# Summing the last output in four column tiles of one bank, with a single output transfer

## The chip, the cores and the metric

One core of one Trainium2 chip. The metric is device time in microseconds (us) of one execution, median over runs. The profile's span, from the first instruction to the last, is about 1.2 us shorter than the device time.

Some words: PE multiplies matrices and sums in PSUM; DVE, ACT and POOL compute on tiles; SP and ACT each have a queue on which they start transfers. The issue is the instruction that starts a transfer, a packet is one piece of it (one row, in the output transfers), the receipt is the increment of a semaphore that says that data has landed. An eviction copies a sum out of PSUM. The tail is the time from the landing of the last weights to the last receipt.

## The reference, cut to what matters

A decode step with a batch of four. An attention over a key and value cache and a small MLP both feed one output of 4 x 576; the MLP ends in a product with w4 (4608 x 576).

```python
xn = _layernorm(x)
# A: q from xn, softmax over the last 2048 keys of the cache, then @ wo
# B: x1 = xn + gather(gelu(_layernorm(xn) @ w1)) @ w2
#    h2 = _gelu(_layernorm(x1) @ w3) @ w4
return x + A(xn, ...) + (x1 + h2)          # [4, 1, 576], bf16
```

What the kernel loads is 88.5 MB, and the last 2048 keys and values of the two caches are 67 MB of it.

## The kernel before

Everything but the small x, which ACT loads, is loaded once, in one long series of transfers on the queue of SP. w4 comes last, in five pieces of 18, 9, 6, 2 and 1 rows per partition, so that the work after the last byte is small. All that goes into the output is summed in two PSUM accumulators of 4 x 288, in column tiles 0 and 32 of the PE array and in two banks; two engines evict them and two queues send them.

```python
W4_ROWS = (18, 9, 6, 2, 1)
out_sb = sb("out_sb", [36, D], BF16)
ACC = [ps[32 * k:32 * k + B, k, 0:HALF] for k in range(2)]      # HALF = 288
...
# output: two transfers of four rows of 576 B, one on either queue
for h, eng in ((0, "sp"), (1, "act")):
    ev_o[h] = add_dma([(o2[:, HALF*h:HALF*(h+1)], out_sb[32*h:32*h+B, HALF*h:HALF*(h+1)])], ("out", h),
                      [f"fin{h}"], 10000, engine=eng)
...
def acc_mm(e, h, lhsT, rhs, start=False, stop=False):
    return e.matmul(ACC[h], lhsT=lhsT, rhs=rhs, start=start, stop=stop, tile_position=(0, 32*h), skip_group_check=True)
...
# one piece of w4: for every row two matmuls of 4 x 288, after its landing
for t in range(t0, t1_):
    for h in hs:
        ins = acc_mm(e, h, h2T_sb[:, t, :], w4tile[t][:, HALF*h:HALF*(h+1)], stop=(t == 35))
...
add("dve", ... tensor_copy(out=out_sb[0:B, 0:HALF], in_=ACC[0]), waits=["MOl0"], sig="fin0")
add("act", ... activation(out=out_sb[32:32+B, HALF:D], in_=ACC[1], func=Copy), waits=["MOl1"], sig="fin1")
```

Of the kernel before, what the change touches and what calls it, by code (L numbers as in the profile page):

```python
# [6 lines left out]
FP32 = mybir.dt.float32  # L7
BF16 = mybir.dt.bfloat16
ACTF = mybir.ActivationFunctionType
# [26 lines left out]
def bass_parallel_sum__sliding_block_cached__mixer_s_mlp__decode_kernel(  # L36
    nc, A_x, A_k_cache, A_v_cache, A_wq, A_wo, B_x, B_w1, B_w2, B_w3, B_w4, out
):
    B, Sq, D = A_x.shape
# [14 lines left out]
    HALF = D // 2  # L54
# [3 lines left out]
    o2 = out.rearrange("b s d -> (b s) d")  # L58

    with ExitStack() as ctx:  # L60
        def sb(name, shape, dt):
            return ctx.enter_context(nc.sbuf_tensor(name, shape, dt))
# [44 lines left out]
        h2T_sb = sb("h2T_sb", [128, 36, B], BF16)  # L107
# [7 lines left out]
        ident_f = sb("ident_f", [128, 128], FP32)  # L115
# [12 lines left out]
        OTy = sb("OTy", [128, B, 32], BF16)  # L128
        ORT = sb("ORT", [128, B, 32], BF16)
        t1 = sb("t1", [B, D], FP32)  # L130
        out_sb = sb("out_sb", [36, D], BF16)

        ps = ctx.enter_context(nc.psum_tensor("ps", [128, 8, 512], FP32))[:]
        Sps = ps[:, 0:4, :]
        tb = [ps[:, 4 + k, :].bitcast(BF16).rearrange("p (t d) -> p t d", t=8) for k in range(4)]
        ACC = [ps[32 * k:32 * k + B, k, 0:HALF] for k in range(2)]
        ORps = ps[:, 2, 0:128]
        rinvps = ps[:, 3, 0:128]
        OTps = ps[:, 6, 0:32]
# [4 lines left out]
        H2Ta = ps[:, 7, :].bitcast(BF16)  # L144
        H2Tb = ps[:, 6, :].bitcast(BF16)[:, 0:128]
# [11 lines left out]
        def add(engine, emit, waits=(), sig=None, key=0.0, inc=(), loop=None, cond=None):  # L157
            seqc[0] += 1
            prog[engine].append(Op(emit, waits, sig, key, seqc[0], inc, loop, cond))

        def tok(nm):
            if nm not in S:
                S[nm] = sem("t_" + "_".join(str(k) for k in (nm if isinstance(nm, tuple) else (nm,))))
            return nm
# [6 lines left out]
        def add_dma(pairs, skey, waits=(), key=0.0, engine="sp"):  # L171
            tok(skey)
            dma_count[skey] = dma_count.get(skey, 0) + 16 * len(pairs)

            def emit(e):
                for o_, i_ in pairs:
                    e.dma_start(o_, i_).then_inc(S[skey], 16)  # L177
            add(engine, emit, waits, None, key)
            return ("dma", skey, dma_count[skey])
# [6 lines left out]
        KT = KV + 40.0  # L186


        P = lambda *a, **k: add("pool", *a, **k)

        def pool_ident(t, tag, pattern, view, key):
            P(lambda e: e.memset(t[:], 1.0), sig=tag + "1", key=key)
            P(lambda e: e.affine_select(out=view, in_=view, compare_op=ALU.is_equal, fill=0.0, base=0,
                                        pattern=pattern, channel_multiplier=1), waits=[tag + "1"], sig=tag, key=key + 0.5)
# [8 lines left out]
        pool_ident(perm_bf, "perm_bf", [[-1, NU], [-NU, NI]], perm_bf[:].rearrange("p (u i) -> p u i", u=NU), -95)  # L203
        pool_ident(permT_bf, "permT_bf", [[-1, NI], [-NI, NU]], permT_bf[:].rearrange("p (i u) -> p i u", u=NU), -95)
        pool_ident(ident_f, "ident_f", [[-1, 128]], ident_f[:], -94)
        P(lambda e: e.memset(hs_inT[:], 0.0), sig="hs_inT", key=-90)
        P(lambda e: e.memset(qs_dummy[:], 0.0), waits=["qs_zero"], inc=[(tok("qs"), 1)], key=-88)
        P(lambda e: e.memset(ones_f[:], 1.0), sig="ones_f", key=-89)
# [3 lines left out]
            waits=["ident_f"], sig="mU", key=-8)  # L212
# [25 lines left out]
        w4tile, w4cols, ev_w4, W4N = [], [], [], []  # L238
# [8 lines left out]
                w4cols.append((base + r, base + 128 * rc, rc))  # L247
            base += 128 * rc
        assert len(w4tile) == 36 and base == F
        ev_o = [None, None]  # L250
        for h, eng in ((0, "sp"), (1, "act")):
            ev_o[h] = add_dma([(o2[:, HALF * h:HALF * (h + 1)], out_sb[32 * h:32 * h + B, HALF * h:HALF * (h + 1)])], ("out", h),
                              [f"fin{h}"], 10000, engine=eng)
            add(eng, lambda e: None, [ev_o[h]], None, 10001)


        def ln_ops(idx, src, dst, first_waits, tag, k0):
# [61 lines left out]
        for b in range(B):  # L319
            add("dve", lambda e, b=b: e.tensor_copy(out=qp_out[:, b], in_=qp_in[:, b]), waits=["qTp", "qpad_zero"],  # L320
                sig="qT" if b == B - 1 else None, key=-29.4)
# [25 lines left out]
        def evac(n):  # L347
            if n % 8 in ACT_EVAC:
                return "act", lambda e: e.activation(out=ktbuf[:, n % 16], in_=tb[n % 4], func=ACTF.Copy)  # L349
            return "dve", lambda e: e.tensor_copy(out=ktbuf[:, n % 16], in_=tb[n % 4])  # L350
# [14 lines left out]
        for c in range(NC):  # L365
            lp = ("K", c // NPOS)
            for k in range(NBLK):
                w = [take(("k", c % NPOS), 16)] if k == 0 else []
                prev = (k + 4) % 8
                w.append(evtok(prev))  # L370
                add("pe", pe_T(NBLK * c + k), waits=w, sig=f"T{NBLK * c + k}", key=NBLK * c + k, loop=lp)
                eng, f = evac(NBLK * c + k)
                add(eng, f, waits=[f"T{NBLK * c + k}"] + ([f"SC{c - 2}"] if c >= 2 else []), inc=[("evA" if eng == "act" else "evD", 1)],
                    key=NBLK * c + k + 0.2)
            add("pe", pe_SC(c - 1), waits=[take("qs")], sig=f"SC{c - 1}", key=NBLK * c + SC_AFTER + 0.5, loop=lp)
            b, gq = CH[c]
            cc = 4 * b + gq
            P(lambda e, c=c, cc=cc: e.tensor_copy(out=Qs[:, c % NPOS, :], in_=Qpad_t[:, 128 * cc:128 * cc + 128]),  # L378
              waits=["qT", "qs_zero"] + ([f"SC{c - NPOS}"] if c >= NPOS - 1 else []), inc=[("qs", 1)], key=c)
# [6 lines left out]
            waits=["rmax"], sig="negb", key=KS + 0.05)  # L386
        for q in range(4):
            add("act", lambda e, q=q: e.activation(out=P_sb[:, q, :], in_=Sps[:, q, :], func=ACTF.Exp,
                                                   bias=negb[:, 0:1], scale=scale, accum_out=rs4[:, q:q + 1]),
                waits=["negb"], sig=f"exp{q}", key=KS + 0.1 + 0.01 * q)  # L390

        for q in range(4):
# [3 lines left out]
                waits=[f"PTx{q}", "permT_bf"] + (["PT0"] if q == 3 else []), sig=f"PTy{q}", key=k0)  # L396
            add("act", lambda e, q=q: e.activation(out=PT_t[:, 512 * q:512 * (q + 1)], in_=ps[:, 4 + q % 3, :], func=ACTF.Copy),
                waits=[f"PTy{q}"], sig=f"PT{q}", key=k0 + 0.16)
# [3 lines left out]
            waits=["rinv", "ident_f"], sig="diag", key=KS + 0.82)  # L402
        add("pe", lambda e: e.matmul(rinvps, lhsT=ones_f[:], rhs=diag[:], start=True, stop=True), waits=["diag", "ones_f", "exp3"],
            sig="rinvp", key=KS + 0.9)
        add("dve", lambda e: e.tensor_copy(out=rinvB[:].rearrange("p (c u e) -> p c u e", u=NU, e=2),
                                           in_=rinvps.rearrange("p (u c e) -> p c u e", u=NU, e=2)),
            waits=["rinvp"], sig="rinvB", key=KS + 1.5)
# [20 lines left out]
        for c in range(NC):  # L428
            w = [f"PV{c - 2}"] if c >= 2 else [f"PT{q}" for q in range(4)] + ["mU_bf1"]
            b, gq = CH[c]  # L430
            add("dve", dve_pad(c), waits=w, inc=[(tok("pad"), 1)], key=KV + 2 * max(c - 1, 0) + 0.2)
            add("pe", pe_PV(c), waits=[take("pad"), take(("v", c % NPOS), 16)] + ([take("otn")] if b == 0 else []), sig=f"PV{c}",
                key=KV + 2 * c, loop=("V", gq))
            if b == B - 1:
                hv = lambda t, gq=gq: t[:, 0:128].rearrange("p (b h) -> p b h", b=B)[:, :, 8 * gq:8 * gq + 8]
                add("dve", lambda e, hv=hv: e.tensor_tensor(out=hv(OTn), in0=OTps.rearrange("p (b h) -> p b h", b=B), in1=hv(rinvB), op=ALU.mult),  # L436
                    waits=["rinvB", f"PV{c}"], sig=f"OTn{gq}" if gq == 3 else None, inc=[(tok("otn"), 1)] if gq < 3 else [], key=KV + 2 * c + 0.1)


        def acc_mm(e, h, lhsT, rhs, start=False, stop=False):  # L440
            return e.matmul(ACC[h], lhsT=lhsT, rhs=rhs, start=start, stop=stop, tile_position=(0, 32 * h), skip_group_check=True)  # L441

# [8 lines left out]
        def pe_AO(half):  # L451
# [10 lines left out]
            waits=["OTy"], sig="ORp", key=KT - 2.5)  # L462
# [34 lines left out]
        for h in range(2):  # L497
# [3 lines left out]
                waits=[f"hs{h}", "ln1"], sig="x1" if h else "x1a", key=-29 + 0.6 * h)  # L501
# [4 lines left out]
        for h in range(2):  # L506
            add("act", lambda e, h=h: e.activation(out=h_sb[:, HALF * h:HALF * (h + 1)], in_=HTps[h], func=ACTF.Gelu_apprx_tanh),
                waits=[f"hT{h}", "x1nT"], sig="gelu_h" if h else None, key=-0.69 + 0.01 * h)

        segs = []  # L510
        for g in range(4):
            t = 9 * g
            while t < 9 * g + 9:
                n = next(m for m, (a, z) in enumerate(W4N) if a <= t < z)
# [18 lines left out]
        for k in range(3):  # L533
            add("act", lambda e, k=k: e.activation(out=h2g[:, 9 * XS[k]:9 * XS[k + 1]], in_=H2ps[k], func=ACTF.Gelu_apprx_tanh), waits=["h2_3"],
                sig="gelu2" if k == 2 else None, key=-0.9 + 0.1 * k)

        def pe_h2T(e):
# [3 lines left out]
            return ins  # L541
        add("pe", pe_h2T, waits=["gelu2"], sig="h2T", key=-0.6)
        h2o = h2T_sb[:].rearrange("p (g j) b -> p g j b", g=4)
        add("act", lambda e: e.activation(out=h2o[:, :, 0:8, :], in_=H2Ta.rearrange("p (j g y) -> p g j y", j=8, g=4)[..., 0:B], func=ACTF.Copy),
            waits=["h2T"], inc=[("evA", 1)], key=-0.3)
        add("dve", lambda e: e.tensor_copy(out=h2o[:, :, 8, :], in_=H2Tb.rearrange("p (g y) -> p g y", g=4)[..., 0:B]),
            waits=["h2T"], inc=[("evD", 1)], key=-0.3)

        last_p = len(W4N) - 1
        for n, (t0, t1_) in enumerate(W4N):  # L550
            def f(e, t0=t0, t1_=t1_, hs=(0, 1), n=n):
                ins = None
                for t in range(t0, t1_):
                    for h in hs:
                        ins = acc_mm(e, h, h2T_sb[:, t, :], w4tile[t][:, HALF * h:HALF * (h + 1)], stop=(t == 35))
                return ins
            if n < last_p:
                add("pe", f, waits=[ev_w4[n]], sig=f"MO{n}", key=KT + 20 + n)
            else:
                for h in range(2):  # L560
                    add("pe", lambda e, f=f, h=h: f(e, hs=(h,)), waits=[ev_w4[n]], sig=f"MOl{h}", key=KT + 20 + n + 0.1 * h)
        add("dve", lambda e: e.tensor_copy(out=out_sb[0:B, 0:HALF], in_=ACC[0]), waits=["MOl0"], sig="fin0", key=KT + 50)  # L562
        add("act", lambda e: e.activation(out=out_sb[32:32 + B, HALF:D], in_=ACC[1], func=ACTF.Copy), waits=["MOl1"], sig="fin1", key=KT + 50)  # L563


        for eng in prog:
            prog[eng].sort(key=lambda op: (op.key, op.seq))
        ev_val = {}
# [91 lines left out]
```

## Time and profile before

| | us |
|---|---|
| device time, median of 6 runs (range) | 214.50 (214.38 to 214.63) |
| span of the profiled run | 213.3 |
| last w4 piece landed | 211.06 |
| both evictions done | 211.88 |
| last output receipt | 213.26 |

The row to keep in mind is the distance between the third and the last: 2.20 us from the last weight byte to the last receipt. Before it the transfers run without a gap. The prediction below shows the slices, the chain and the last ten microseconds.

### The profile page before, as it was taken

How to read it: one execution, taken by the hardware profiler on the slowest of the kernel's cores; microseconds unless marked ns; L12 is line 12 of the kernel's file. 1: busy time of each engine (PE TensorE's matmuls, PEld its weight loads, DVE VectorE, ACT ScalarE, POOL GpSimd, SP SyncE). 2: the span in 40 equal slices, each digit the busy share in tenths (PEclk: the TensorE clock that was granted, in tenths of full speed). 3: DMA queues.
4: the chain of work that ended last, by engine and by line, in shares of the span. 5: the costliest groups of instructions: out<-in, count | busy, mean ns of one | idle time of the engine just before them, and what ended most of it. 6: DMA issues, size and time to landing. Idle time of an engine off the chain costs nothing. (4 is left out here: it accounts for less than half of the span.)

```text
span 213.3 us, 5930 instructions
## 1 busy us (share of the span) xinstructions
PE 143.1 (67%) x2679; PEld 110.1 (52%) x2679; DVE 75.3 (35%) x148; ACT 61.6 (29%) x76; POOL 10.9 (5%) x38
## 2 busy tenths in 40 slices
PE   0048469999999999999996377133434433336995
PEld 0023246887788878888774067133434433334542
DVE  0242700767666666666664830100010001001000
ACT  2001204566556666666656620000000000000000
POOL 8300000000010000000000000000000000000000
PEclk9999959999999999999999555555555555555799
DMA  7999999999999999999999999999999999999993
GB/s 289 413 389 480 422 406 427 424 429 424 430 427 427 433 427 427 426 430 430 424 433 427 421 440 417 421 433 427 424 424 433 427 424 433 430 426 437 426 405 131
DMA packets 6446, 88.65 MB, mean 416 GB/s; under 512 B 744, under 2 KB 884, under 8 KB 1444
## 3 DMA queue, kind: packets, MB, share of 16 engines
q1 hardware_dynamic: 6420, 88.50, 97.8%
q8 instruction: 8, 0.13, 0.2%
q14 instruction: 2, 0.02, 0.0%
q10 hardware_dynamic: 16, 0.01, 0.0%
HBM read 88.49 MB, written 0.00 MB: 415 GB/s over the span
## 5 line engine op out<-in xcount | busy, mean ns | idle before, releaser
L343 PE MATMUL ps<-perm_bf,ring 128*128 128x128 bf16 x1024 | 62.1, 219 | 0.9
L343 PEld LDWEIGHTS ps<-perm_bf,ring 128*128 128x128 bf16 x1024 | 57.5, 98 | 9.6 <-issue 9.4
L350 DVE COPY kt<-ps 128x1024 bf16<-128x1024 bf16 x80 | 52.3, 687 | 26.1 <-PE ps L343 25.9
L349 ACT ACTIVATE kt<-ps 128x1024 bf16<-128x1024 bf16 x48 | 48.9, 1025 | 30.1 <-PE ps L343 28.9
L424 PE MATMUL ps<-PTpad,ring 128*128 128x8 bf16 x1024 | 29.7, 168 | 41.3 <-PEq L586 37.6
L424 PEld LDWEIGHTS ps<-PTpad,ring 128*128 128x128 bf16 x1024 | 28.7, 104 | 42.5 <-issue 42.4
L563 ACT ACTIVATE out_sb<-ps 4x288 bf16<-4x288 f32 x1 | 0.4, 403 | 87.4 <-PE ps L441 87.4
L357 PE MATMUL ps<-kt,Qs 128*32 128x512 bf16 x272 | 17.8, 382 | 1.4 <-PEq L586 1.4
L413 DVE TENSOR_TENSOR PTpad<-PT,mU_bf 128x512 bf16<-128x512 bf16 x16 | 6.4, 422 | 30.1 <-PE ps L424 30.1
L436 DVE TENSOR_TENSOR OTn<-ps,rinvB 128x32 bf16<-128x32 f32 x4 | 0.8, 192 | 33.9 <-PE ps L424 33.9
L279 PE MATMUL ps<-ident_bf,xn_bf 4*128 4x4 bf16 x8 | 0.6, 170 | 13.7 <-DVE ragsrc L273 13.7
L357 PEld LDWEIGHTS ps<-kt,Qs 128*32 128x32 bf16 x272 | 5.7, 95 | 6.8 <-issue 1.5
L378 POOL COPY Qs<-Qpad 128x128 bf16<-128x128 bf16 x16 | 4.6, 296 | 86.4 <-PE ps L357 72.4
L279 PEld LDWEIGHTS ps<-ident_bf,xn_bf 4*128 4x128 bf16 x8 | 0.4, 112 | 13.7 <-issue 11.3
L525 PE MATMUL ps<-w,x1nT 128*32 128x387 bf16 (+7 forms) x90 | 6.0, 411 | 2.1 <-DMA w<-in_B_w_dram 1.8
L525 PEld LDWEIGHTS ps<-w,x1nT 128*32 128x32 bf16 x90 | 4.6, 126 | 3.4 <-DMA w<-in_B_w_dram 2.1
L441 PE MATMUL ps<-w,ORT 128*4 128x288 bf16 x64 | 5.5, 344 | 0.4 <-DVE ORT L463 0.4
L562 DVE CAST out_sb<-ps 4x288 bf16<-4x288 f32 x1 | 0.4, 445 | 14.5 <-PE ps L441 14.5
L441 PE MATMUL ps<-w,h2T_sb 128*4 128x288 bf16 x72 | 5.0, 286 | 0.6 <-DMA w<-in_B_w_dram 0.6
L395 PE MATMUL ps<-kt,permT_bf 128*128 128x512 bf16 x4 | 2.4, 608 | 4.3 <-DVE kt L394 4.1
L263 ACT ACTIVATE sd<-mv 4x1 f32<-4x1 f32 x3 | 0.6, 203 | 14.5 <-DVE mv L261 14.5
L441 PEld LDWEIGHTS ps<-w,ORT 128*4 128x4 bf16 x64 | 3.2, 102 | 2.9 <-DVE ORT L463 1.0
(102 smaller groups left out, 65.7 us busy)
## 6 DMA issues: line engine op xcount, KB each, us to landing
ring<-in_A_k_cache_dram SPq DMA_DIRECT2D x16, 2048.0 KB, 14.4
ring<-in_A_v_cache_dram SPq DMA_DIRECT2D x16, 2048.0 KB, 17.4
w<-in_B_w_dram SPq DMA_DIRECT2D x1, 4608.0 KB, 24.1
w<-in_A_wo_dram SPq DMA_DIRECT2D x2, 2304.0 KB, 21.0
kt<-in_A_wq_dram SPq DMA_DIRECT2D x1, 4096.0 KB, 13.2
w<-in_B_w_dram SPq DMA_DIRECT2D x1, 2592.0 KB, 28.0
w<-in_B_w_dram SPq DMA_DIRECT2D x3, 576.0 KB, 14.2
w<-in_B_w_dram SPq DMA_DIRECT2D x1, 1296.0 KB, 30.6
```

The lines of the kernel that those rows point to most:

```text
L279: e.transpose(XTps[idx][:, r, :], v[:, r, :], ident_bf[0:B, 0:B])
L343: ins = e.transpose(tb[n % 4][:, t, :], slot_t(c)[:, 8 * k + t, :], perm_bf[:])
L349: return "act", lambda e: e.activation(out=ktbuf[:, n % 16], in_=tb[n % 4], func=ACTF.Copy)
L350: return "dve", lambda e: e.tensor_copy(out=ktbuf[:, n % 16], in_=tb[n % 4])
L357: ins = e.matmul(Sps[32 * u:32 * u + 32, q, :].rearrange("p (t i) -> p t i", t=16), lhsT=Qs[:, c % NPOS, 32 * u:32 * u + 32], rhs=ktgrp[:, ...
L378: P(lambda e, c=c, cc=cc: e.tensor_copy(out=Qs[:, c % NPOS, :], in_=Qpad_t[:, 128 * cc:128 * cc + 128]), waits=["qT", "qs_zero"] + ([f"SC{ ...
L395: add("pe", lambda e, q=q: e.matmul(ps[:, 4 + q % 3, :], lhsT=permT_bf[:], rhs=PTx[:, q, :], start=True, stop=True), waits=[f"PTx{q}", "pe ...
L413: return lambda e: e.tensor_tensor(out=PTpad[:, c % 2], in0=PTv[:, :, cc, :].unsqueeze(2).to_broadcast([128, NT, NU, 2]), in1=mU_bf[:].uns ...
L424: ins = e.matmul(o_, lhsT=slot_t(c)[:, t, :], rhs=PTpad[:, c % 2, t].rearrange("p u e -> p (u e)"), start=(t == 0), stop=(t == NT - 1))
L436: add("dve", lambda e, hv=hv: e.tensor_tensor(out=hv(OTn), in0=OTps.rearrange("p (b h) -> p b h", b=B), in1=hv(rinvB), op=ALU.mult), waits ...
L441: return e.matmul(ACC[h], lhsT=lhsT, rhs=rhs, start=start, stop=stop, tile_position=(0, 32 * h), skip_group_check=True)
L525: ins = e.matmul(H2ps[k][32 * g:32 * g + 32, :].rearrange("p (x c) -> p x c", c=9)[:, :, off:off + cnt], lhsT=x_, rhs=w[:, base_:base_ + 1 ...
```

## The change

Intent: shorten the work after the last byte. From the second w4 piece on, each row is four matmuls of 144 columns in the four column tiles, all in bank 7, so that one short cast evicts everything and one transfer sends it. The sum so far (attention, residuals, first piece) is copied to SBUF and folded into the new accumulators by four fp32 products with a selection matrix. So that the four batch rows of tile k fall on partitions 32k + 0, 8, 16, 24, the weights are padded with zeros to 32 columns, which takes a second layout of h2 (h2W).

```diff
-        out_sb = sb("out_sb", [36, D], BF16)
+        out_sb = sb("out_sb", [128, D // 4], BF16)
+        accS = sb("accS", [B, 2, HALF], FP32)
+        selF = sb("selF", [B, 32], FP32)
+        h2W = sb("h2W", [128, 2, 9, 32], BF16)
+        ACC4 = [ps[32 * k:32 * k + 32, 7, 0:QUART] for k in range(4)]      # QUART = 144
...    (memsets of h2W and selF on POOL; two copies of h2 into h2W[..., 0:32:8])
-        for h, eng in ((0, "sp"), (1, "act")):
-            ev_o[h] = add_dma([(o2[:, HALF*h:HALF*(h+1)], out_sb[32*h:32*h+B, HALF*h:HALF*(h+1)])], ("out", h), ...)
+        ev_o = add_dma([(o2.rearrange("b (k n) -> k b n", k=4), out_sb[0:128:8, :])], "out", ["fin"], 10000)
...
+        add("dve", ... tensor_copy(out=accS[:, 0, :], in_=ACC[0]), waits=["MO0"], sig="accS0")
+        add("act", ... activation(out=accS[:, 1, :], in_=ACC[1], func=Copy), waits=["MO0"], sig="accS1")
+            for k in range(4):            # the fold
+                ins = acc4_mm(e, k, selF[:], accS[:, k // 2, QUART*(k % 2):QUART*(k % 2 + 1)], start=True)
...            for t in range(t0, t1_):    # pieces 2 to 5
+                    for k in range(4):
+                        ins = acc4_mm(e, k, h2W[:, t // 9 - 2, t % 9, :], w4tile[t][:, QUART*k:QUART*(k+1)], stop=(t == 35))
-        (two evictions of 4 x 288)
+        add("dve", ... tensor_copy(out=out_sb[:], in_=ps[:, 7, 0:QUART]), waits=[last piece], sig="fin")
```

More of the change, by code (lines that the diff above doesn't have):

```diff
@@ L136, in bass_parallel_sum__sliding_block_cached__mixer_s_mlp__decode_kernel @@
         ACC = [ps[32 * k:32 * k + B, k, 0:HALF] for k in range(2)]
+        QUART = D // 4
+        ACC4 = [ps[32 * k:32 * k + 32, 7, 0:QUART] for k in range(4)]
         ORps = ps[:, 2, 0:128]
@@ L205, in bass_parallel_sum__sliding_block_cached__mixer_s_mlp__decode_kernel @@
         pool_ident(ident_f, "ident_f", [[-1, 128]], ident_f[:], -94)
+        P(lambda e: e.memset(h2W[:], 0.0), sig="h2W_zero", key=-91)
+        P(lambda e: e.memset(selF[:], 0.0), sig="selF_zero", key=-87.5)
+        P(lambda e: e.tensor_copy(out=selF[:, 0:32:8], in_=ident_f[0:B, 0:B]), waits=["selF_zero", "ident_f"], sig="selF", key=-87)
         P(lambda e: e.memset(hs_inT[:], 0.0), sig="hs_inT", key=-90)
@@ L249, in bass_parallel_sum__sliding_block_cached__mixer_s_mlp__decode_kernel @@
         assert len(w4tile) == 36 and base == F
-        ev_o = [None, None]
-        for h, eng in ((0, "sp"), (1, "act")):
-            ev_o[h] = add_dma([(o2[:, HALF * h:HALF * (h + 1)], out_sb[32 * h:32 * h + B, HALF * h:HALF * (h + 1)])], ("out", h),
-                              [f"fin{h}"], 10000, engine=eng)
-            add(eng, lambda e: None, [ev_o[h]], None, 10001)
+        ev_o = add_dma([(o2.rearrange("b (k n) -> k b n", k=4), out_sb[0:128:8, :])], "out", ["fin"], 10000)
+        add("sp", lambda e: None, [ev_o], None, 10001)
         def ln_ops(idx, src, dst, first_waits, tag, k0):
@@ L543, in bass_parallel_sum__sliding_block_cached__mixer_s_mlp__decode_kernel @@
         h2o = h2T_sb[:].rearrange("p (g j) b -> p g j b", g=4)
+        add("act", lambda e: e.activation(out=h2W[:, :, 0:8, 0:32:8], in_=H2Ta.rearrange("p (j g y) -> p g j y", j=8, g=4)[:, 2:4, :, 0:B], func=ACTF.Copy),
+            waits=["h2T", "h2W_zero"], sig="h2Wa", key=-0.32)
+        add("dve", lambda e: e.tensor_copy(out=h2W[:, :, 8, 0:32:8], in_=H2Tb.rearrange("p (g y) -> p g y", g=4)[:, 2:4, 0:B]),
+            waits=["h2T", "h2W_zero"], sig="h2Wd", key=-0.32)
         add("act", lambda e: e.activation(out=h2o[:, :, 0:8, :], in_=H2Ta.rearrange("p (j g y) -> p g j y", j=8, g=4)[..., 0:B], func=ACTF.Copy),
@@ L547, in bass_parallel_sum__sliding_block_cached__mixer_s_mlp__decode_kernel, with pe_mo0 @@
             waits=["h2T"], inc=[("evD", 1)], key=-0.3)
-        last_p = len(W4N) - 1
-        for n, (t0, t1_) in enumerate(W4N):
-            def f(e, t0=t0, t1_=t1_, hs=(0, 1), n=n):
+        def pe_mo0(e):
+            ins = None
+            for t in range(*W4N[0]):
+                for h in range(2):
+                    ins = acc_mm(e, h, h2T_sb[:, t, :], w4tile[t][:, HALF * h:HALF * (h + 1)])
+            return ins
+        assert W4N[0] == (0, 18)
+        add("pe", pe_mo0, waits=[ev_w4[0]], sig="MO0", key=KT + 20)
@@ new lines, in bass_parallel_sum__sliding_block_cached__mixer_s_mlp__decode_kernel, with acc4_mm, pe_fold @@
+        add("dve", lambda e: e.tensor_copy(out=accS[:, 0, :], in_=ACC[0]), waits=["MO0"], sig="accS0", key=KT + 30)
+        add("act", lambda e: e.activation(out=accS[:, 1, :], in_=ACC[1], func=ACTF.Copy), waits=["MO0"], sig="accS1", key=KT + 30)
+        def acc4_mm(e, k, lhsT, rhs, start=False, stop=False):
+            return e.matmul(ACC4[k], lhsT=lhsT, rhs=rhs, start=start, stop=stop, tile_position=(0, 32 * k), skip_group_check=True)
+        def pe_fold(e):
+            ins = None
+            for k in range(4):
+                ins = acc4_mm(e, k, selF[:], accS[:, k // 2, QUART * (k % 2):QUART * (k % 2 + 1)], start=True)
+            return ins
@@ L552, in f @@
+        add("pe", pe_fold, waits=["accS0", "accS1", "selF", "h2Wa", "h2Wd"], sig=None, key=KT + 20.8)
+        for n, (t0, t1_) in enumerate(W4N[1:], 1):
+            def f(e, t0=t0, t1_=t1_):
                 ins = None
                 for t in range(t0, t1_):
-                    for h in hs:
-                        ins = acc_mm(e, h, h2T_sb[:, t, :], w4tile[t][:, HALF * h:HALF * (h + 1)], stop=(t == 35))
-                return ins
-            if n < last_p:
-                add("pe", f, waits=[ev_w4[n]], sig=f"MO{n}", key=KT + 20 + n)
-            else:
-                for h in range(2):
-                    add("pe", lambda e, f=f, h=h: f(e, hs=(h,)), waits=[ev_w4[n]], sig=f"MOl{h}", key=KT + 20 + n + 0.1 * h)
@@ L562, in bass_parallel_sum__sliding_block_cached__mixer_s_mlp__decode_kernel @@
-        add("dve", lambda e: e.tensor_copy(out=out_sb[0:B, 0:HALF], in_=ACC[0]), waits=["MOl0"], sig="fin0", key=KT + 50)
-        add("act", lambda e: e.activation(out=out_sb[32:32 + B, HALF:D], in_=ACC[1], func=ACTF.Copy), waits=["MOl1"], sig="fin1", key=KT + 50)
+                    for k in range(4):
+                        ins = acc4_mm(e, k, h2W[:, t // 9 - 2, t % 9, :], w4tile[t][:, QUART * k:QUART * (k + 1)], stop=(t == 35))
+                return ins
+            add("pe", f, waits=[ev_w4[n]], sig=f"MO{n}", key=KT + 20 + n)
@@ L566, in bass_parallel_sum__sliding_block_cached__mixer_s_mlp__decode_kernel @@
+        add("dve", lambda e: e.tensor_copy(out=out_sb[:], in_=ps[:, 7, 0:QUART]), waits=[f"MO{len(W4N) - 1}"], sig="fin", key=KT + 50)
         for eng in prog:
```

## The prediction

> **What bounds the kernel now.** I read the page's slices first, then the chain that ended last, then the last ten microseconds in order of time, and last the groups that the change replaces.
>
> The slices (each is 213.3/40 = 5.33 us) of the kernel before:
>
> ```profile
> PEclk9999959999999999999999555555555555555799
> DMA  7999999999999999999999999999999999999993
> GB/s 289 413 389 480 422 406 427 424 429 424 430 427 427 433 427 427 426 430 430 424 433 427 421 440 417 421 433 427 424 424 433 427 424 433 430 426 437 426 405 131
> ```
>
> From the second slice to the last but one the 16 DMA engines are busy over 90% and move about 427 GB/s. The transfers bound the kernel, and only work that lies after the last weight byte can show in the time. The chain confirms it:
>
> ```profile
> 177.79 32.21 DMA w<-in_B_w_dram
> 210.00 0.04 issue
> 210.04 1.40 PE ps L441 x18
> 211.44 0.43 DVE out_sb L562
> ```
>
> The chain view puts the last 18 matmuls down as 1.40 us of PE work. The timeline shows that this is too simple:
>
> ```profile
> 204.91 2.37 PE L441 MATMUL ps<-w,h2T_sb 128*4 128x288 bf16 x36 [0.26 <-DMA w<-in_B_w_dram]
> 207.21 1.25 PE L447 MATMUL ps<-zeros_bf 128*128 128x512 bf16 x5
> 208.39 1.27 PE L441 MATMUL ps<-w,h2T_sb 128*4 128x288 bf16 x18
> 210.04 1.35 PE L441 MATMUL ps<-w,h2T_sb 128*4 128x288 bf16 x18 [0.38 <-DMA w<-in_B_w_dram]
> 211.10 0.09 PEld L441 LDWEIGHTS ps<-w,h2T_sb 128*4 128x4 bf16 x2 [0.24 <-DMA w<-in_B_w_dram]
> 211.43 0.45 DVE L562 CAST out_sb<-ps 4x288 bf16<-4x288 f32 x1 [14.52 <-PE ps L441]
> 211.46 0.40 ACT L563 ACTIVATE out_sb<-ps 4x288 bf16<-4x288 f32 x1 [87.38 <-PE ps L441]
> 211.89 0.28 ACTq L177 DMA_DIRECT2D out_dram<-out_sb  x1
> 211.90 0.30 SPq L177 DMA_DIRECT2D out_dram<-out_sb  x1
> ```
>
> The 18 matmuls belong to three weight pieces of 6, 2 and 1 rows. The trace's semaphore records have the pieces landing at 207.96 (9 rows), 210.00, 210.70 and 211.06 us. The last two weight loads start at 211.10, 0.24 us after the loads before them ended, so they wait for the last piece and not for the PE. After 211.06 the path is: last two matmuls (semaphores at 211.403 and 211.438), eviction (both done by 211.883), DMA issue, output packets, receipt (213.264), end at 213.28. That tail of 2.2 us is all that the change can touch at the end.
>
> ```profile
> SPq L592 <- DMA out_dram<-out_sb: 1.1, 1, 1.1
> ```
>
> SP spends half of it, 1.1 us, waiting for its 2.2 KB output after the issue.
>
> **What the Trainium skill says.** "DMA: Bandwidth & Descriptors", section "Why a DMA increments its semaphore by 16 and not by 1": the number of engines is the largest up to 16 that divides the slowest dimension of both sides. The trace agrees: each output transfer of 4 rows shows 4 packets of 576 B and four late increments. The new transfer has 16 partitions on one side but [4, 4, 144] in DRAM, so by this rule it still uses 4 engines, with four packets of 288 B each. The same page's "Specifications" says that transfers under 512 B are read-modify-written; packets fall from 576 to 288 B, and no row of this trace shows a 288 B write. "TensorEngine Tiling (Array Packing)", "Theoretical Speedup": at most 32 columns of weights allow up to 4x. The trace agrees: the score matmuls, four tiles in one bank, ran 16 of 512 columns in 1.05 us; less some 0.17 us of pipeline (382 ns for one less 512/2.4 = 213) that is 55 ns each, a quarter of 213. "TensorE: Matmul & The Clock Gate", "Back-to-back issue gap", gives an issue floor of about 25 ns; no group at full clock here shows it.
>
> **The change, part by part.**
>
> Setup. POOL gets two memsets and a 4x4 copy. A 128x512 memset took 525 ns, so 128x576 is near 0.59 us. It precedes the hs_inT memset, which ends at 6.87 us while its user starts at 20.37: hidden. ACT and DVE each get one copy of h2 at 36.1 us, estimated at no more than the 278 and 167 ns of the present ones. The tokens behind them are wanted by the third and fourth groups of key transposes, about 37.5 and 38.0 us (four groups of eight from 36.56, 1.95 us in all), and would come at about 36.4 and 36.6: hidden. Even if not, the fifth key transfer is issued at 41.61 while the fourth lands at 50.43, so 8.8 us are spare before the queue runs dry.
>
> Middle. The first piece stays at 36 matmuls of 288 columns in two tiles, done at 207.29. Two new evictions of 4x288, 445 and 403 ns like today's, end near 207.77. Five filler matmuls keep PE until about 208.30, so the copies are hidden. Then come four fp32 products of 144 columns. Today's fp32 pair of 288 columns in two tiles took 0.65 us for four records; half the columns, twice the tiles: 0.24 + 0.17 = 0.41 us if the tiles overlap, about 1.0 us if none do. Then 36 matmuls of 144 columns: 144/2.4/4 = 15 ns each in four tiles, 25 ns at the skill's floor, so 0.54 to 0.90 us. Piece two ends at 208.30 + 0.24 + 0.9 + 0.17 = 209.6 at worst with overlap, 210.3 if fp32 is serial; the next piece lands at 210.00. The 6-row piece then is 24 x 25 = 0.6 us and ends issuing at 210.64, before the next lands at 210.70. The last piece meets an idle PE. I choose "no loss, no gain here": the matmul count and speed are covered by the landings.
>
> End. Last piece: four matmuls of 144 columns. One of 288 took 284 ns from its start at 211.105, so 144 take 284 - 60 = 224, and the last, started some 10 ns later, would signal at about 211.38 with today's 45 ns of delay. DVE starts near 211.41 instead of 211.43. Eviction: one DVE cast of 128x144 instead of 4x288 on each of two engines.
>
> ```profile
> L562 DVE CAST out_sb<-ps 4x288 bf16<-4x288 f32 x1 | 0.4, 445 | 14.5 <-PE ps L441 14.5
> L463 DVE CAST ORT<-ps 128x128 bf16<-128x128 f32 x1 | 0.3, 291 | 0.9 <-PE ps L461 0.9
> ```
>
> The same cast of 128 columns on 128 partitions took 291 ns: partitions cost nothing, and (445 - 291)/160 = 0.96 ns per column gives 291 + 16 x 0.96 = 306 ns. Done at 211.73 rather than 211.883: **gain 0.15 us**.
>
> Output. Today SP issues at 211.899 for 303 ns, its first packet moves 0.54 us after the issue ended, ACT's 0.48 us after its own. The eight packets start one after another, ACT's at 212.654 to 212.721, SP's at 212.746 to 212.814, about 22 ns apart, so SP's wait behind ACT's for 92 ns. One transfer alone does not queue: **gain 0.06 to 0.09 us**. Against it: 16 packets rather than 4. At 22 ns apart they add 12 x 22 = 0.26 us; if the four engines feed in parallel, four packets of some 25 ns each add 0.08 us. I take 0.16. The issue handles more elements in one more dimension: issues of 128 rows took 432 ns, key transfers with three dimensions 535, the 4-row output 303, so 16 elements cost perhaps 0.03 us more. Narrow, 32-byte-aligned writes: I put 0.03 us. **Loss 0.22 us.**
>
> Sum: -0.15 - 0.08 + 0.22 = -0.01 us by the middle of each; with the ends from -0.15 - 0.09 + 0.08 = -0.16 to -0.15 - 0.06 + 0.26 + 0.10 + 0.10 = +0.25. I lean to the parallel feed, as four engines each have their own packets, and predict -0.06: 214.52 - 0.06 = **214.46 us**.
>
> **The rivals.**
> 1. PE is the real limit at the end, as the chain view has it (1.40 us for 18 matmuls). Then halving it would save 0.5 us or more: about 213.9. Against it: the 0.24 us stop before the last loads, and the landings at 210.70 and 211.06.
> 2. The output transfer becomes the wait: 16 small packets fed serially and read-modify-written, with a late receipt. Then the gain of the eviction is eaten and more: 214.7 to 214.9. The 22 ns spacing speaks for it; the trace has no such packet to decide.
> 3. The fold lands on the path: serial fp32 and a clock fallen to half. PE then finishes piece three late; but with 0.4 us of slack per landing a loss over 0.3 us, to 214.8, would take both. The clock table grants full speed from 199.84 to 213.5 us.
> 4. The early copies shift the key stream. With 8.8 us spare, zero.
>
> **Range and chances.** The terms above span -0.16 to +0.25; run-to-run spread of before is 0.13 us. So 214.15 to 214.80. A 2% change is 4.3 us, more than the whole 2.2 us tail; faster by that is as good as excluded, slower only if the stream of transfers is disturbed.
>
> **What would show it.** Right: last piece still landing near 211.06; the last four weight loads behind a DMA wait; a 128x144 cast of about 306 ns ended by 211.75; 16 packets of 288 B on the SP queue with the last receipt near 213.2; the fold done before 209 us. Wrong: matmuls without a wait before the last piece, a fold over 1 us, a cast over 0.4 us, more than 1.3 us between the issue's end and the last receipt, or a gap in the transfers before 204 us.

## More of the kernel before

One more view turns out to matter. It is the timeline of the two queues in the first microseconds: start, duration of the issuing instruction, destination and source.

```profile
0.81 0.41 SPq L177 DMA_DIRECT2D w<-in_B_w_dram  x1
1.27 0.41 SPq L177 DMA_DIRECT2D kt<-in_A_wq_dram  x1
1.72 0.54 SPq L177 DMA_DIRECT2D w<-in_B_w_dram  x1
2.31 0.69 SPq L177 DMA_DIRECT2D w<-in_A_wq_dram  x1
2.34 0.56 ACTq L177 DMA_DIRECT2D x_sb<-in_A_x_dram  x1
```

The first two load 128 neighbouring partitions, the next two 64 rows onto every second partition: half the rows, yet a longer issue. I did not read this before I predicted. It is a hint and no more: in the same microseconds ACT's load of x, four plain rows on neighbouring partitions, took 0.56 us too.

## The result, and the profile after

| | before | after |
|---|---|---|
| device time, median of 6 (range), us | 214.50 (214.38 to 214.63) | 214.70 (214.62 to 214.86) |
| ratio | | 1.001 (95%: 0.9997 to 1.0023) |
| last w4 landing to last output receipt, us | 2.20 | 2.42 |

Ratios are the mean time of one kernel's runs over that of the other's of the same rounds, so not quite the ratio of the medians. The 0.2 us between the medians is at the edge of what the runs resolve, but the traces show it too: the tail is 0.22 us longer. The three traces that hold the changed kernel's own tail have it at 2.42 to 2.43 us, and the two of the old tail both at 2.20.

The slices of the changed kernel, for the transfers and their rate:

```profile
DMA  7999999999999999999999999999999999999993
GB/s 289 412 391 463 435 402 430 424 431 427 427 421 430 430 433 416 433 433 424 430 427 436 421 434 423 427 424 427 433 427 424 424 436 430 424 433 430 431 406 118
```

They are as before: nothing disturbed the stream. The wait of SP for its output is, too, at first sight:

```profile
SPq L613 <- DMA out_dram<-out_sb: 1.1, 1, 1.1
```

But this wait begins only when the issue has ended, and a longer issue does not show in it. The chain that ended last:

```profile
178.17 32.47 DMA w<-in_B_w_dram
...
210.69 0.31 PE ps L570 x8
...
211.04 0.28 PE ps L570 x4
...
211.34 0.31 DVE out_sb L586
```

The chain now stays with the transfers until the 2-row piece, 0.65 us longer than before, and counts 0.59 us of PE instead of 1.40. This looks like a gain of 0.8 us of PE work, and the time shows none of it: the chain merely hands to the DMA what it gave to the PE before. The timeline of the end:

```profile
208.31 0.45 PE L570 MATMUL ps<-accS,selF 4*32 4x144 f32 x8
208.69 0.75 PE L570 MATMUL ps<-w,h2W 128*32 128x144 bf16 x36
209.97 0.56 PE L570 MATMUL ps<-w,h2W 128*32 128x144 bf16 x24 [0.54 <-DMA w<-in_B_w_dram]
211.04 0.10 PEld L570 LDWEIGHTS ps<-w,h2W 128*32 128x32 bf16 x4 [0.23 <-DMA w<-in_B_w_dram]
211.34 0.31 DVE L586 CAST out_sb<-ps 128x144 bf16<-128x144 f32 x1 [3.65 <-PE ps L570]
211.68 0.64 SPq L182 DMA_DIRECT2D out_dram<-out_sb  x1
```

The fold takes 0.45 us behind the fillers and is over before 209 us. The PE is 0.54 us idle before the third piece instead of 0.38, and still waits before the last. The cast takes 0.31 us as computed. The last line is the surprise: the issue of the one output transfer takes 0.64 us, where the two before took 0.28 and 0.30, side by side.

The trace's semaphore and packet records split the tail, in us:

| part of the tail | before (SP's half, which ended last) | after | difference |
|---|---|---|---|
| last w4 landing to eviction done | 0.821 | 0.661 | -0.160 |
| issue of the output transfer | 0.303 | 0.637 | +0.334 |
| end of issue to first packet | 0.544 | 0.635 | +0.091 |
| first to last packet | 0.095 | 0.123 | +0.028 |
| last packet to last receipt | 0.423 | 0.349 | -0.074 |
| sum, with 0.02 between eviction and issue | 2.20 | 2.42 | +0.22 |

The eviction gained its 0.16 us; the output transfer cost 0.38 us.

### The profile page after: what moved, and what is told of

It reads as the page before. It is cut to its first block, busy times and chain, and to the rows that moved or that the text cites. A ratio compares the mean times of both kernels' runs of the same rounds, so it can differ in the third digit from the quotient of the medians.

```text
span 213.5 us, 6021 instructions
## 1 busy us (share of the span) xinstructions
PE 140.3 (66%) x2719; PEld 110.3 (52%) x2723; DVE 75.6 (35%) x150; ACT 61.4 (29%) x77; POOL 11.6 (5%) x41
## 5 line engine op out<-in xcount | busy, mean ns | idle before, releaser
L348 PE MATMUL ps<-perm_bf,ring 128*128 128x128 bf16 x1024 | 61.4, 219 | 0.9 <-PEq L607 0.5
L354 ACT ACTIVATE kt<-ps 128x1024 bf16<-128x1024 bf16 x48 | 48.3, 1024 | 29.8 <-PE ps L348 29.2
L530 PE MATMUL ps<-w,x1nT 128*32 128x387 bf16 (+7 forms) x90 | 6.8, 437 | 2.8 <-DMA w<-in_B_w_dram 2.5
L400 PE MATMUL ps<-kt,permT_bf 128*128 128x512 bf16 x3 | 1.8, 607 | 4.9 <-DVE kt L399 4.8
L446 PE MATMUL ps<-w,ORT 128*4 128x288 bf16 x64 | 4.7, 310 | 0.4 <-DVE ORT L468 0.4
```

Source lines behind the costliest of these rows:

```text
L348: ins = e.transpose(tb[n % 4][:, t, :], slot_t(c)[:, 8 * k + t, :], perm_bf[:])
L354: return "act", lambda e: e.activation(out=ktbuf[:, n % 16], in_=tb[n % 4], func=ACTF.Copy)
L400: add("pe", lambda e, q=q: e.matmul(ps[:, 4 + q % 3, :], lhsT=permT_bf[:], rhs=PTx[:, q, :], start=True, stop=True), waits=[f"PTx{q}", "pe ...
L530: ins = e.matmul(H2ps[k][32 * g:32 * g + 32, :].rearrange("p (x c) -> p x c", c=9)[:, :, off:off + cnt], lhsT=x_, rhs=w[:, base_:base_ + 1 ...
```

## The experiments

What is special in the new transfer? Three things differ from the old: the packets are narrower (288 B), the source rows lie 8 partitions apart, and the DRAM side has three dimensions ([4, 4, 144]). It also has 16 packets instead of 4. My first theory was the three dimensions alone. Eleven kernels were run, in five groups.

### 1. Shapes by themselves, first series

The changed kernel, with nine more output transfers after its own, each waiting for the one before, so that issue and packets can be read undisturbed.

```diff
-        ev_o = add_dma([(o2.rearrange("b (k n) -> k b n", k=4), out_sb[0:128:8, :])], "out", ["fin"], 10000)
+        shapes = [(o3, out_sb[0:128:8, :], "sp"), (o3, out_sb[0:128:8, :], "sp"), (o3[0:2], out_sb[0:64:8, :], "sp"), ...]
+        for i, (o_, i_, eng) in enumerate(shapes):
+            ev_o = add_dma([(o_, i_)], ("out", i), [ev_o], 10000 + i, engine=eng)
```

> The changed kernel, followed by nine more output transfers, one after another, each waiting for the one before; only their issue durations and packets are read. Order: the changed shape [4,4,144] again; half of it [2,4,144]; one quarter [4,144]; four 288 B packets to one row; 16 packets of 288 B with one stride [16,144]; four of 576 B (as before the change); four of 1152 B; the last two on the other queue: four of 1152 B, and [4,4,144]. Theory (the three-dimensional shape with four engines costs the issue): [4,4,144] again about 0.64 us, [2,4,144] about 0.45, every shape with one stride about 0.30, [16,144] among them about 0.32. Rival A (number of packets costs): [16,144] also about 0.64, [2,4,144] 0.41. Rival B (cost of the first use of a shape or a queue state): the second [4,4,144] falls to about 0.3. Rival C (packets under 512 B cost): [4,144] also over 0.4.

The output was correct; the theory was not. Issue in ns, and us from its end to the first packet:

| transfer | issue | first packet |
|---|---|---|
| [4,4,144], its own | 644 | 0.635 |
| [4,4,144] again | 601 | 0.640 |
| [2,4,144] | 520 | 0.642 |
| [4,144], 8 apart | 657 | 0.641 |
| 4 x 288 B to one row, 32 apart | 516 | 0.646 |
| [16,144], one stride, 8 apart | 537 | 0.659 |
| 4 x 576 B | 312 | 0.465 |
| 4 x 1152 B | 269 | 0.479 |
| 4 x 1152 B, ACT's queue | 283 | 0.479 |
| [4,4,144], ACT's queue | 645 | 0.646 |

The theory of the three dimensions alone fell: [4,144] and [16,144] have one stride in DRAM and are as slow. So did the number of packets (4 and 16 cost alike), the first use, and the queue. What stayed: the slow ones are all of 288 B, and all from partitions 8 or 32 apart.

### 2. The transfer in its place, and the PE

Three kernels ran on the same chip as the first series.

Two queues: the changed kernel with its output in two transfers of eight packets each.

```diff
+        for h, eng in ((0, "sp"), (1, "act")):
+            ev_o = add_dma([(o2[:, HALF*h:HALF*(h+1)].rearrange("b (k n) -> k b n", k=2), out_sb[64*h:64*h+64:8, :])], ("out", h), ...)
```

> The changed kernel with its output in two transfers, eight packets of 288 B each, one on either queue. Theory (the long issue of one transfer is the loss): issue about 0.45 us each in parallel, so about 0.2 us less than the changed kernel, 214.5 us, as the kernel before. Rival (narrow packets and their receipt are the loss, not the issue): stays at 214.7.

215.21 us, ratio 1.0024 (1.0011 to 1.0038) to the kernel before: worse, not better. Both expectations missed. The timeline of its end:

```profile
211.83 0.62 SPq L182 DMA_DIRECT2D out_dram<-out_sb  x1
211.83 0.64 ACTq L182 DMA_DIRECT2D out_dram<-out_sb  x1
```

Each half is as slow to issue as the whole. The issues ran side by side, but the packets stand in line: SP's first moves 0.638 us after its issue ended, ACT's 0.970. So a second slow transfer costs about as much again, as a wait before its packets: the tail grew from 2.42 to 2.72 us.

One row: the kernel before with both halves evicted to the same four partitions and one transfer of four rows of 1152 B.

```diff
+        ev_o = add_dma([(o2, out_sb[0:B, :])], "out", ["fin0", "fin1"], 10000)
-        add("act", ... activation(out=out_sb[32:32 + B, HALF:D], in_=ACC[1], func=Copy) ...)
+        add("act", ... activation(out=out_sb[0:B, HALF:D], in_=ACC[1], func=Copy) ...)
```

> The kernel before with both halves evicted to the same four partitions and one transfer of four rows of 1152 B. Theory (two transfers contend at the end; a single transfer of four packets has a short issue): 0.1 to 0.15 us under the kernel before, 214.37. Rival (the receipt alone sets the end): 214.5, the same.

214.58 us beside 214.60, ratio 0.9996 (0.9983 to 1.0010): the same. A single transfer is not slow as such: issue 303 ns, first packet 0.472 us later. Against SP's half of before it saves 0.07 us to the first packet and 0.09 in the receipt, but packets of 1152 B take 0.179 us from first to last instead of 0.095, and the issue, which waits for both evictions, starts 0.05 later after the landing. The tail is 2.18 us against 2.20. My 0.1 to 0.15 us was too much; the time is that of the rival, though nothing here shows that the receipt alone sets it.

Half the PE work: the kernel before with every second row of the 9-row and 6-row pieces left out.

```diff
-                for t in range(t0, t1_):
+                for t in range(t0, t1_, 2 if n in (1, 2) else 1):
```

> The kernel before with every second row of the 9-row and 6-row pieces left out of the matmuls (wrong result on purpose). Theory (PE waits for each landing): the same time, within 0.1 us. Rival (the last matmuls bound the end, as the chain view has it): 0.3 us or more faster.

214.53 us, ratio 0.9994 (0.9981 to 1.0008), tail 2.20 us, as expected. The PE does not bound the end. The sum is wrong, though the comparison passes it: the dropped rows are within its tolerance.

### 3. Shapes, second series, and the transfer undone

The same kind of chain, behind the kernel before, with size and distance of partitions varied apart from each other.

```diff
+        shapes = [(o2[:, 0:144], x_sb[:, 0:144]), (o2[:, 0:288], zeros_bf[0:4, 0:288]), (o2[:, 0:288], zeros_bf[0:32:8, 0:288]), ...]
```

> The kernel before, its output sent last, after ten other transfers in a chain; only issue durations and packets are read. Order: 4 x 288 B from neighbouring partitions of the input tile; 4 x 576 B from a zero tile, neighbouring partitions, then the same from partitions 8 apart; 4 x 288 B from neighbouring partitions of the zero tile, then 8 apart; 4 x 512 B; 4 x 256 B; 4 x 320 B; 8 x 576 B neighbouring, then 8 apart; then the real output in two halves. Theory S (packets under 512 B lengthen the issue): all of 288, 256 and 320 B take 0.5 us or more and start 0.63 us after it, neighbouring or not; 512 and 576 B take about 0.3 and 0.47, 8 apart too. Theory P (partitions that are not neighbours lengthen it): every one 8 apart takes 0.5 or more, also at 576 B; every neighbouring one 0.3, also at 256 to 320 B. Theory A (a row size that is no multiple of 64 B): 288 B slow, 256, 320, 512 and 576 B fast.

The output was correct. The issues of the second to the fifth transfer on SP's queue (4 x 576 B neighbouring and 8 apart, then 4 x 288 B neighbouring and 8 apart):

```profile
213.17 0.26 SPq L177 DMA_DIRECT2D out_dram<-zeros_bf  x1
214.36 0.69 SPq L177 DMA_DIRECT2D out_dram<-zeros_bf  x1
216.13 0.25 SPq L177 DMA_DIRECT2D out_dram<-zeros_bf  x1
217.27 0.64 SPq L177 DMA_DIRECT2D out_dram<-zeros_bf  x1
```

First packets came 0.474, 0.633, 0.476 and 0.635 us after. 256, 320 and 512 B from neighbours took 253, 253 and 258 ns; eight of 576 B took 276 ns from neighbours, 602 ns 8 apart. Width does not matter at these sizes, distance does. From issue to last receipt the four take 1.17, 1.75, 1.13 and 1.69 us. Theory P held against S and A.

The transfer undone, the sum kept: four casts to the same four partitions and one transfer of 1152 B rows.

```diff
-        add("dve", ... tensor_copy(out=out_sb[:], in_=ps[:, 7, 0:QUART]) ...)
+        for k in range(4):      # k < 2 on DVE, else on ACT
+            add(eng, ... copy(out=out_sb[:, QUART*k:QUART*(k+1)], in_=ps[32*k:32*k+B, 7, 0:QUART]) ...)
+        ev_o = add_dma([(o2, out_sb[:])], "out", ["fin1", "fin3"], 10000)
```

> The changed kernel with its transfer undone: the four tiles are evicted by four casts of 4x144 (two on each engine) to the same four partitions, and one transfer of four rows of 1152 B sends them. Theory (the transfer is the whole loss): the eviction takes 0.5 to 0.6 us instead of 0.31, the issue 0.30 instead of 0.64 and the first packet 0.47 after it instead of 0.64, so about 0.2 us under the changed kernel, 214.5. Rival (the sum in four tiles costs time itself): stays at 214.7.

> The changed kernel as it is, on the chip of the run beside it. Both theories: 0.15 to 0.25 us over the kernel before.

On one chip: before 214.60, undone 214.58 (0.9997, 0.9983 to 1.0010), changed kernel 214.71 (1.0005, 0.9991 to 1.0019). The runs put the undone one below the changed one by 0.13 us, their ranges overlap by 0.05; its trace has the eviction at 0.63 us from first cast to last, the issue at 303 ns and the tail at 2.31 us against 2.43.

```profile
212.13 0.30 SPq L182 DMA_DIRECT2D out_dram<-out_sb  x1
```

Against the kernel before, the sum in four tiles costs and gains nothing that the runs resolve, though this one trace, of the slowest of the five runs, has the tail 0.11 us above 2.20. The changed kernel was 0.11 us over the one before this time, less than the 0.15 I had expected at least.

### 4. Neighbouring partitions

If distance is the whole cost, the layout can be mended: rows of even tiles on the last four partitions of their quadrant and of odd tiles on the first four, which makes eight neighbours of each half (28 to 35, 92 to 99).

```diff
+                ins = acc4_mm(e, k, h2W[:, t // 9 - 2, t % 9, 28*(k % 2):28*(k % 2) + 32], ...)      # h2W is 60 wide, data at 28:32
+            ev_o = add_dma([(o2[:, HALF*h:HALF*(h+1)].rearrange("b (k n) -> k b n", k=2), out_sb[64*h+28:64*h+36, :])], ...)
```

> The changed kernel with the four output rows of even tiles put on the last four partitions of their quadrant and those of odd tiles on the first four, so that each half of the output lies on eight neighbouring partitions; one transfer of eight packets of 288 B on either queue. Theory P (the distance of 8 partitions is the whole cost): issues of about 0.30 us instead of 0.62 to 0.64, first packets about 0.48 and 0.55 after, last w4 landing to the end about 1.95 us against 2.20 in the kernel before and 2.44 in the changed one, so 214.35, 0.3 us or more under the changed kernel and 0.2 under the one before. Rival (a destination of three dimensions is slow of itself): issues over 0.45 us, time 214.5 or more.

> The same two transfers from partitions 8 apart, on the same chip as the run beside it. Theory P: about 0.8 us over it, 215.15: two slow issues that also stand in line. Rival: no more than 0.2 us over it.

215.32 us (1.0029, 1.0015 to 1.0043) and 215.09 (1.0021, 1.0008 to 1.0035). The mended one, expected 0.8 us under the other, is 0.23 us over it:

```profile
211.89 0.71 SPq L182 DMA_DIRECT2D out_dram<-out_sb  x1
211.90 0.74 ACTq L182 DMA_DIRECT2D out_dram<-out_sb  x1
```

Neighbouring partitions, and the longest issues of all. "Distance is the whole cost" fell. Either three dimensions in DRAM are slow too, or a run that starts at 28 and crosses partition 32 is.

### 5. The two conditions apart

> The kernel before, its output sent last, after ten other transfers in a chain, from a zero tile. Order: [8,288] to one stride from partitions 28 to 35; [4,144] from 28 to 31; [4,144] from 1 to 4; eight packets from partitions 0 to 7 to [2,4,144]; the same to [4,2,144]; sixteen from 0 to 15 to [4,4,144]; sixteen from 0 to 15 with one stride; four of 576 B from partitions 2 apart; two from partitions 8 apart; one from partition 8. Theory D (two separate conditions, each slow alone: partitions that are not neighbours, or a DRAM side of three dimensions): rows 4, 5, 6 and 8, 9 at 0.5 to 0.7 us with first packets over 0.6 us after; rows 1, 2, 3, 7 and 10 at 0.3 or less and 0.48. Theory Q (a start that is no multiple of 32, or a run across partition 32, made the last miss): rows 1, 2 and 3 slow, rows 4 to 6 fast.

```diff
+        shapes = [(q2, zeros_bf[28:36, 0:288]), (o2[:, 0:144], zeros_bf[28:32, 0:144]), (o2[:, 0:144], zeros_bf[1:5, 0:144]),
+                  (o3[0:2], zeros_bf[0:8, 0:144]), ...]
```

The ten issues on SP's queue, in the order of the expectation:

```profile
212.06 0.33 SPq L177 DMA_DIRECT2D out_dram<-zeros_bf  x1
213.32 0.26 SPq L177 DMA_DIRECT2D out_dram<-zeros_bf  x1
214.50 0.25 SPq L177 DMA_DIRECT2D out_dram<-zeros_bf  x1
215.65 0.72 SPq L177 DMA_DIRECT2D out_dram<-zeros_bf  x1
217.44 0.70 SPq L177 DMA_DIRECT2D out_dram<-zeros_bf  x1
219.21 0.62 SPq L177 DMA_DIRECT2D out_dram<-zeros_bf  x1
220.96 0.34 SPq L177 DMA_DIRECT2D out_dram<-zeros_bf  x1
222.30 0.63 SPq L177 DMA_DIRECT2D out_dram<-zeros_bf  x1
224.01 0.60 SPq L177 DMA_DIRECT2D out_dram<-zeros_bf  x1
225.63 0.24 SPq L177 DMA_DIRECT2D out_dram<-zeros_bf  x1
```

Theory D as put down, but for sizes just outside its ranges (0.33 and 0.34 us for rows 1 and 7, 0.72 for row 4): rows 4, 5, 6 (three dimensions in DRAM, from neighbours) and 8, 9 (one stride in DRAM, partitions 2 and 8 apart) are slow, with first packets 0.627 to 0.645 us after; rows 1, 2, 3, 7 and 10 are fast, with 0.468 to 0.490. A start at partition 28 or 1 does not make it slow (328, 264 and 253 ns). Either condition alone does (605 and 634 ns by distance, 622 to 721 by dimensions), and both together are no slower (601 to 645 ns for [4,4,144] in the first series). Why three dimensions cost 0.3 us or more on these small stores, but only 0.10 on key loads of 128 rows (535 against 432 ns), is not shown.

Last, four transfers of two dimensions from neighbours, two on either queue:

```diff
+            ev_o = add_dma([(o2[:, QUART*k:QUART*(k+1)], out_sb[32*k:32*k+B, :]) for k in (2*h, 2*h+1)], ("out", h), ["fin"], 10000, engine=eng)
```

> The changed kernel with its output rows on four neighbouring partitions of each quadrant and four transfers [4,144], two on either queue, each with two dimensions. Theory D: four fast issues, the second on each queue done 0.56 us after the eviction, first packets 0.48 later; the landing of the last w4 piece to the end 2.15 to 2.2 us, as before the change: 214.5. Theory Q gives the same. If the number of transfers were the cost instead: 214.8 or more.

214.80 us, ratio 1.0009 (0.9997 to 1.0022): a miss of 0.3 us, and the time that was put down for the case that the number of transfers is the cost. The issues are fast, 302 and 295 ns on SP, 277 and 310 on ACT, as theory D has it, but two in a row last as long as one slow one, and SP's last receipt came 0.505 us after its last packet, where single transfers show 0.32 to 0.37. The tail is 2.39 us. In the kernel before, the later of two transfers also had the longer receipt (0.423 against ACT's 0.329). Why receipts are longer when two queues finish together stays open.

## Why the prediction came out as it did

The time, 214.70, lies in the range of 214.15 to 214.80; the point, 214.46, was 0.24 us low and on the wrong side of the kernel before (214.52 was the median of the three runs known then). That the range held was in part luck: the issue alone cost 0.33 us more, where the range had +0.25 for all terms together, and cheaper packets and an earlier receipt brought the time back.

- "The transfers bound the kernel, and only work that lies after the last weight byte can show" was right. The rate did not move.
- "No loss, no gain here" for the middle was right. With half of the matmuls of two pieces gone (group 2) the time stood; the fold took 0.45 us against 0.41 computed, and the 36 matmuls of 144 columns started in rounds of four every 62.5 ns, 15.6 ns each, at the low end of the 15 to 25 ns assumed. Rival 1, that the PE is the real limit, is refuted; the chain view alone would have misled here.
- Eviction, "gain 0.15 us": measured 0.16. The cast took 308 ns against 306.
- Setup hidden: right in effect, wrong in two sizes. The copies into h2W took 456 ns on ACT and 195 on DVE, not "no more than the 278 and 167". With 8 us spare it does not show.
- Output: here the sum failed. The mis-sized term is "16 elements cost perhaps 0.03 us more" for the issue; it was +0.33 us. I had drawn it from the 535 ns of the key transfers, the 432 of plain loads of 128 rows and the 303 of the 4-row output, as if both rows and the third dimension cost in proportion to the elements. On these small stores the cost is one of form: partitions that are not neighbours, or three dimensions in DRAM, at 516 to 737 ns for 2 to 16 packets, against 243 to 335 for the plain form at 1 to 16.
- "One transfer alone does not queue: gain 0.06 to 0.09 us" was not there to be had: the slow form also delays the first packet, by 0.09 us against SP's before, which had stood in line, and by 0.15 to 0.16 against one that had not.
- The packets, +0.16 predicted, cost 0.03: the four DMA engines worked side by side. Narrow writes, +0.03, cost nothing (4 x 288 B from neighbours landed 1.13 to 1.17 us after the issue began, 4 x 576 B 1.16 to 1.21). These two misses, and a receipt 0.07 us earlier, hid part of the first.
- Rival 2, a slow output transfer at 214.7 to 214.9, is what came, but by another mechanism: neither serial packets nor a cost of narrow writes nor a late receipt, but the issue.
- None of the signs of being wrong that I listed came: the one on the output counts from the issue's end (1.11 us to the last receipt, under the 1.3), and the loss lay in the issue itself.

No version tried beats the kernel before by what the runs resolve; the one-row transfer is level with it. That the short cast and a fast transfer can be had together is not shown; they would need the 16 rows on neighbouring partitions with one stride in DRAM, which the column tiles, 32 partitions apart with a quarter of the columns each, do not give as they are laid out here.

## What to carry to other kernels

A tail after the last load is a sum of small fixed costs: read each from the trace, the issue of the last transfer included, before trading one for another. A shorter eviction that forces an awkward layout on the output transfer can lose more at the issue than it gains. Check the form of a transfer against issues of the same form that the trace already holds, even at its other end: here the loads onto every second partition, at 0.54 and 0.69 us, hinted at it. A hint has to be tested by itself, as the plain load of 0.56 us beside them shows.

## What the Trainium skill lacked or had wrong

- "DMA: Bandwidth & Descriptors" counts descriptor generation as small and sequencer dispatch as about 50 ns ("Anatomy of one DMA — SWDGE (gpsimd) path"), for another issuing path; it does not say how the time of an issue from SP or ACT depends on the form of the transfer. The runs show, for stores of at most 16 packets, 243 (one packet) to 335 ns (16) from neighbouring partitions with at most two dimensions, and 516 to 737 ns from partitions 2, 8 or 32 apart or with three dimensions in DRAM, no more for 16 packets (537 to 645) than for two to eight.
- The same page's "Latency and other measured facts" has about 600 ns to the first byte and does not say from what moment. For a transfer alone the runs show 0.465 to 0.490 us from the end of the issue in the fast form and 0.627 to 0.659 in the slow one; from its start 0.72 to 0.83 and 1.16 to 1.35.
- The same page's "Issuing engines are not separate DMA queues" says that issuing from several engines saves only the sequencer's time. The runs agree, and give the wait that is left, for which it has no size: of two slow issues side by side (0.62 and 0.64 us) the first packets moved 0.64 and 0.97 us after the issues.
- The same page's "Specifications" warns of read-modify-write under 512 B. For four packets of 256 to 320 B the runs show no cost: 1.13 to 1.17 us from issue to last receipt, beside 1.16 to 1.21 for 512 and 576 B.
- "TensorE: Matmul & The Clock Gate", "Back-to-back issue gap", gives a floor of about 25 ns for one matmul after another; that it does not hold from one column tile to the next is not said there. In four column tiles four matmuls of 144 columns started every 62.5 ns, 15.6 ns each; its formula N/2.4 + 2.5 (62.5 ns here) holds for the round of four.
